# Block-sparse attention into a softplus feed-forward on one Trainium2 core: attention's pieces at five places of a feed-forward step in place of two

## The chip, the cores and the metric

One core of one Trainium2 chip. The metric is the device time of one execution in microseconds (us), the median of the runs shown. TensorE (PE in the profile) multiplies, VectorE (DVE) and ScalarE (ACT) work on elements, GpSimd (POOL) does so too and issues gathers, and SyncE (SP) issues most transfers.

## The reference

Attention over 4 batches, 8 heads, 768 positions and 64 values a head. A query block of 32 sees the key blocks beside it, the first and the last block, and three sampled ones; queries of the first and the last block see all. Its output is the input of a feed-forward pair with softplus between, with weights given as float64:

```python
def _attn_ref(q, k, v, sampled_blocks):
    scores = scale * np.matmul(q, k.transpose(0, 1, 3, 2))
    mask = np.abs(blk_i - blk_j) <= window
    mask = mask | (blk_i == 0) | (blk_j == 0) | (blk_i == n_blocks - 1) | (blk_j == n_blocks - 1)
...
    attn = np.exp(scores)
    attn = attn / (np.sum(attn, axis=-1, keepdims=True) + 1e-09)
    return np.matmul(attn, v)

def _moe_ref(x, w_in, w_out):
    h = x @ w_in
    g = np.maximum(h, 0.0) + np.log1p(np.exp(-np.abs(h)))
    return g @ w_out
```

x has 3072 rows of 512, w_in is 512 x 2048, w_out 2048 x 512.

## The kernel before

The rows of x are cut into 8 blocks of 384 (three groups of 128), the 2048 hidden columns into 16 slices of 128. A **feed-forward step** j is one row block t with one slice f. Steps 0 to 47 take slices 0 to 5 of all row blocks (phase 0) and leave partial sums in DRAM; steps 48 to 127 take slices 6 to 15 (phase 1) and add them. In a step `hidden` (line 230) makes twelve matmuls of 128x384: for each of four parts of the contraction high times high (L237), high weight times low input (L238), low times high (L239), since every float32 is held as a high and a low float32r half. ScalarE and VectorE make softplus of it over the next two steps, and three steps later (LEAD) `project` (line 284) makes nine output matmuls of 128x512, three for each group of rows (L293 to L295).

Attention is 28 sets (24 groups of four query blocks, and 4 sets of the blocks that see all keys) in two units each. A unit has three **pieces** (`pieces`, line 764): scores (L597 or L621; VectorE reads them out with a minimum, L603, L628), values (exponents on ScalarE, L653, for a later unit, then the matmuls L696 or L710), and transposes (L666, copied out by ScalarE L673 or VectorE L671). A set's output is turned (L741) and split into the high and low halves of x. For a set, keys are copied together: neighbours by VectorE (L493), the first and last block, called end keys, by `end_keys` (L476), sampled ones by GpSimd (L507). There are two buffers of gathered keys, two of values, four of PSUM with the tag "s", which the hidden tile, score tiles, transposes and turned outputs share, and three of PSUM for the outputs.

The float64 weights come as 64-bit integers (`load`, L148, 512 KB each) and are made float32 in small ticks between the pieces (`convert`, line 868): two ScalarE operations (L155, L159), three VectorE ones (L165, L172, L178) and an addition on GpSimd (L182). Slices 0 to 5 are split into halves at once (L189, L196); later ones go to DRAM (L201) and come back when attention's memory is free (`load_w2`, L897), where `split_w2` (line 899) makes the halves: a cast on ScalarE (L902) and a subtraction on GpSimd (L903).

Order: SP issues in program order. The other engines' order is set by a scheduler that goes by the program's order where it can. The program's order is the main loop from line 906: `first_half(j)` (L265 cast, L256 logarithm, hidden matmuls), then pieces as many as `due(j + 0.5)` asks for, then `second_half(j)` (L261, L271, the softplus rounding L248, L250, L251, and `project`), then pieces up to `due(j + 1.0)`. Three pieces come to a step. Before step 0 all pieces of the first row block run by themselves; with them, and until slices 0 to 5 are converted, ticks come at EARLY_TICKS = 1 for each piece and half step, later at LATE_TICKS = 0.5. `store` (line 306) copies a finished row block of outputs (`os`, L312) out of PSUM, on ScalarE and VectorE in turn.

Of the kernel before, what the change touches and what calls it, by code (L numbers as in the profile page):

```python
# [8 lines left out]
F32 = mybir.dt.float32  # L9
# [6 lines left out]
ALU = mybir.AluOpType  # L16
# [11 lines left out]
EARLY = 6  # L28

GROUPS = 3  # L30

LEAD = 3
# [18 lines left out]
def sparse_attention_ffn(  # L51
# [178 lines left out]
    def hidden(n):  # L230
        phase, t, f = seq[n]
        wh, wl = W[0, f]
        ph = ps_s.tile([P, 512], F32, tag="s", name=f"h{n}")[:, 0:TB]
        hi, lo = (X[phase, t][:, i] for i in range(2))
        for c in range(NC):
            cols = slice(c * P, (c + 1) * P)
            nc.tensor.matmul(ph, wh[:, cols], hi[:, c], start=(c == 0), stop=False)  # L237
            nc.tensor.matmul(ph, wh[:, cols], lo[:, c], start=False, stop=False)  # L238
            nc.tensor.matmul(ph, wl[:, cols], hi[:, c], start=False, stop=(c == NC - 1))  # L239
        e = gp.tile([P, TB], F32, tag="e", name=f"e{n}")  # L240
        nc.scalar.activation(e, ph, AF.Abs)  # L241
        nc.scalar.activation(e, e, AF.Exp, scale=-1.0)  # L242
        E[n] = (e, ph)
# [40 lines left out]
    def project(n):  # L284
        phase, t, f = seq[n]
        first, last = (f == (0, EARLY)[phase]), (f == (EARLY, NF)[phase] - 1)
        wh, wl = W[1, f]
        gh, gl = G.pop(n)
        for m in range(GROUPS):
            if first:  # L290
                po[m] = ps_o.tile([P, DM], F32, tag="o", name=f"o{phase}{t}_{m}")
            cols = slice(m * P, (m + 1) * P)
            nc.tensor.matmul(po[m], gh[:, cols], wh, start=first, stop=False)  # L293
            nc.tensor.matmul(po[m], gh[:, cols], wl, start=False, stop=False)  # L294
            nc.tensor.matmul(po[m], gl[:, cols], wh, start=False, stop=last)  # L295
        if last:
            store(phase, t)

# [139 lines left out]
    def load_queries(m):  # L438
        if m >= len(order):
            return  # L440
        b, g = order[m]
        qc[b, g] = wk.tile([P, NP, NI, BLOCK], F32, tag="qc", name=f"qc{b}_{g}", bufs=2)
        nc.sync.dma_start(out=qc[b, g], in_=q[b, g])
# [29 lines left out]
    def end_keys(m, copies):  # L473

        for copy, slot, blkno in zip(copies, (NR, 2 * NR + 1), (0, LAST)):
            copy(  # L476
                out=kg[m % 2][:, :, slot, :],
                in_=kT[order[m][0]][:, blkno : blkno + 1, :].to_broadcast([P, NI, NP * BLOCK]),
            )

    def gather_keys(m):
        b, g = order[m]
        ni = NI if g < NG - 1 else 2
        kd = kg[m % 2]

        def of_block(i):

            eng = (nc.vector if i < 2 else nc.scalar) if m == 0 else nc.gpsimd
            copy = nc.scalar.copy if m == 0 and i >= 2 else eng.tensor_copy
            if i == 0:  # L490
                at = kT[b][:, 4 * g : 4 * g + NR, :]
                pattern = [list(x) for x in at.ap]
                ins = nc.vector.tensor_copy(  # L493
                    out=kd[:, 0:ni, 0:NR, :].rearrange("p i s f -> p i (s f)"),
                    in_=bass.AP(at.tensor, at.offset, [pattern[0], [NP * BLOCK, ni], [1, NR * NP * BLOCK]]),
                )
                tc.keep_in_program_order(ins)
                if m % NG < 2:
                    first = nc.vector.tensor_copy if m == 0 else nc.scalar.copy
                    end_keys(m, (first, nc.scalar.copy) if m < 2 else 2 * (nc.gpsimd.tensor_copy,))  # L500
            (r,) = registers(eng, [2 * g + i // 2])
            for s in range(NR):
                x = nc.s_assert_within(
                    eng.snap((r >> (16 * (i % 2) + 5 * s)) & 31), 0, LAST,
                    skip_runtime_bounds_check_because="a sampled block is one of the key blocks",
                )
                copy(  # L507
                    out=kd[:, i, 1 + NR + s, :], in_=kT[b][:, bass.ds(x, 1), :].rearrange("p n f -> p (n f)")
                )

        key_work.extend((m, lambda i=i: of_block(i)) for i in range(ni))


# [328 lines left out]
    load_values(1)  # L842
    load_keys(2)
    scores(1)
    for h in range(weights.extra):
        weights.load(h)
    exponents(0)
    load_queries(2)
    transposes(0)
    exponents(1)  # L850
    spread_ends()
# [6 lines left out]
    def attend():  # L858
        nonlocal done
        attention[done]()  # L860
        done += 1
        gather()
        convert()
# [20 lines left out]
    def due(x):  # L884

        last, at = 0.0, needs[0]
        for t in range(1, NTB):
            end = t * EARLY - AHEAD
            if x <= end:
                return at + (needs[t] - at) * (x - last) / (end - last)  # L890
            last, at = end, needs[t]
        return len(attention)

    def load_w2(f):
        for which in range(2):
            W[which, f] = [pools["w2"].tile([P, DM], F32R, name=f"w{x}{which}{f}") for x in range(2)]
            nc.sync.dma_start(out=W[which, f][1].bitcast(F32), in_=wD[which, f])  # L897

    def split_w2(f, which):

        hi, lo = W[which, f]
        nc.scalar.copy(out=hi, in_=lo.bitcast(F32))  # L902
        nc.gpsimd.tensor_tensor(out=lo, in0=lo.bitcast(F32), in1=hi.bitcast(F32), op=ALU.subtract)  # L903

    ahead = None
    for j in range(len(seq) + LEAD):
        if j >= SECOND:
            t, f = seq[j][1:] if j < len(seq) else (NTB, -1)
            if f == EARLY + 2 and t + 1 < NTB:
                load_x(t + 1)  # L910
            if f == EARLY + 4:
                load_y(t)
        if j == SECOND - 3:
            load_x(0)
        first_half(j)
        while done < len(attention) and done < due(j + 0.5):
            attend()
        convert()
        second_half(j)
        while done < len(attention) and done < due(j + 1.0):  # L920
            attend()
        convert()
        if done == len(attention) and ahead is None:
            assert weights.done(), weights.at
            actx.close()
            pools["w2"] = ctx.enter_context(tc.tile_pool(name="w2", bufs=1, side="right"))
            ahead = EARLY
        while ahead is not None and ahead < min(NF, EARLY + 2 * (j + EARLY - SECOND + 1)):
            load_w2(ahead)
            ahead += 1  # L930

        for which in range(2):
            f = EARLY + j + 3 - SECOND - LEAD * which
            if EARLY <= f < NF:
                split_w2(f, which)


_BLOCKS = 24
# [35 lines left out]
```

## Time and profile before

| | before |
|---|---|
| median of 3 runs | 823.24 us (821.51 to 823.3) |
| the profiled execution, its own time | 830.36 us |
| its span, first to last instruction | 828.6 us |
| TensorE busy | 786.3 us (95%), 8108 matmuls |
| VectorE busy | 587.6 us (71%) |
| ScalarE busy | 485.8 us (59%) |
| GpSimd busy | 261.6 us (32%) |
| mean granted TensorE clock | 0.983 |
| HBM read, written | 97.85 MB, 30.41 MB |

Busy time is the time in which an engine works on at least one instruction. TensorE's matmuls overlap, so one that shows 0.34 us can be followed after 0.17 us: its pace is read from the starts. The shares are means over stretches with different limits, so stretches are looked at apart. The profiled execution took longer than the runs behind the median; differences are worked out within it.

### The profile page before, as it was taken

What the parts mean: (1) busy time and instruction counts of PE and PEld (TensorE: products, weight loads), DVE (VectorE), ACT (ScalarE), POOL (GpSimd) and SP (SyncE); (2) the same over time, 40 slices, a digit from 0 to 9 for tenths busy, and PEclk for the clock granted to TensorE, in tenths of its full rate; (3) what the DMA queues carried; (4) which work ended last, traced back from release to release, by engine and by line L of the source; (5) the groups of instructions that cost most, each with busy time, mean ns of one, the idle gap of its engine ahead of it and who ended that gap; (6) DMA issues with size and microseconds to landing.
All of it is one profiled execution on the core that took longest, in us unless ns stands there. A gap on an engine that the chain in (4) does not pass through costs nothing.

```text
span 828.6 us, 21424 instructions
## 1 busy us (share of the span) xinstructions
PE 786.3 (95%) x8108; PEld 651.7 (79%) x8108; DVE 587.6 (71%) x1454; ACT 485.8 (59%) x1170; POOL 261.6 (32%) x421
## 2 busy tenths in 40 slices
PE   8779969999999999999999999999999999999997
PEld 7546747776778767776778779999999999999996
DVE  5678999688787788886664886666656565656564
ACT  4776856766776766765664664444444444444442
POOL 6683886442666328464000670000000000000000
PEclk9799989999999999999999999999999999999999
DMA  8877698577697686955515461212121222222021
GB/s 246 237 221 265 199 243 290 173 236 251 183 296 224 215 278 181 286 147 167 204 40 190 143 240 64 102 52 97 57 88 65 77 76 77 77 77 77 0 77 39
DMA packets 48408, 129.66 MB, mean 156 GB/s; under 512 B 5488, under 2 KB 5616, under 8 KB 46256
## 3 DMA queue, kind: packets, MB, share of 16 engines
q1 hardware_dynamic: 42304, 109.79, 41.6%
q0 software_dynamic: 5712, 17.57, 7.5%
q8 instruction: 64, 1.05, 0.5%
q10 hardware_dynamic: 288, 0.93, 0.3%
q14 instruction: 40, 0.33, 0.1%
HBM read 97.85 MB, written 30.41 MB: 155 GB/s over the span
## 4 chain that ended last, share of the span: by engine, by line
PE 61%; DVE 18%; ACT 11%; issue 5%; DMA 3%; SPq 1%; another core or an unknown queue 1%; DVEq 0%; ACTq 0%
PE h L237 9%; PE o L293 8%; PE h L238 8%; PE h L239 8%; PE o L294 8%; PE o L295 8%; ACT pr L653 5%; PE t L666 3%; PE s L597 3%; PE x L696 3%; DVE e L250 2%; DVE pr L603 2%; DVE u L248 2%; DMA vg<-in_v_dram 2%; DVE wt L178 1%
## 5 line engine op out<-in xcount | busy, mean ns | idle before, releaser
L237 PE MATMUL h<-x,w 128*128 128x384 f32 x512 | 178.5, 349 | 4.4 <-DVE e L251 2.5
L238 PE MATMUL h<-x,w 128*128 128x384 f32 x512 | 173.9, 340 | 0.0
L239 PE MATMUL h<-x,w 128*128 128x384 f32 x512 | 173.5, 339 | 0.0
L293 PE MATMUL o<-w,gh 128*128 128x512 f32 x384 | 156.1, 407 | 2.9 <-DVE os L312 2.8
L248 DVE TENSOR_SCALAR u<-e 128x384 f32<-128x384 f32 x128 | 51.5, 402 | 145.3 <-ACT e L242 145.3
L295 PE MATMUL o<-w,gl 128*128 128x512 f32 x384 | 152.2, 396 | 0.0
L294 PE MATMUL o<-w,gh 128*128 128x512 f32 x384 | 151.7, 395 | 0.0
L241 ACT ACTIVATE e<-h 128x384 f32<-128x384 f32 x128 | 62.8, 491 | 126.2 <-PE h L239 125.8
L653 ACT ACTIVATE pr<-pr,nmax 128x256 f32<-128x256 f32 (+2 forms) x208 | 110.3, 532 | 44.0 <-DVE nmax L603 27.9
L237 PEld LDWEIGHTS h<-x,w 128*128 128x128 f32 x512 | 97.3, 190 | 14.8 <-DVE e L251 2.8
L265 ACT CAST gh<-u 128x384 fp32r<-128x384 f32 x128 | 65.4, 511 | 73.8 <-PE o L294 67.1
L563 POOL DMA_INDIRECT vg<-in_v_dram,ix x88 | 88.4, 1004 | 58.5 <-PE x L696 30.3
L238 PEld LDWEIGHTS h<-x,w 128*128 128x128 f32 x512 | 97.6, 191 | 3.6
L507 POOL COPY kg<-kT 128x128 f32 x252 | 84.9, 382 | 49.2 <-PE s L597 47.0
L239 PEld LDWEIGHTS h<-x,w 128*128 128x128 f32 x512 | 97.2, 190 | 0.0
L256 ACT ACTIVATE u<-u 128x384 f32<-128x384 f32 x128 | 66.9, 523 | 50.2 <-DVE e L250 41.5
L293 PEld LDWEIGHTS o<-w,gh 128*128 128x128 f32 x384 | 72.0, 188 | 24.8 <-issue 8.6
L295 PEld LDWEIGHTS o<-w,gl 128*128 128x128 f32 x384 | 72.1, 188 | 17.3
L603 DVE CUSTOM_DVE_ANT_1 pr<-s,mask 128x256 f32<-128x256 f32 (+1 forms) x192 | 69.6, 415 | 22.0 <-PE s L597 10.5
L250 DVE SCALAR_TENSOR_TENSOR e<-u,e 128x384 f32<-128x384 f32 x128 | 82.2, 642 | 3.8
L294 PEld LDWEIGHTS o<-w,gh 128*128 128x128 f32 x384 | 72.2, 188 | 13.4 <-issue 1.2
L261 DVE TENSOR_TENSOR u<-u,e 128x384 f32<-128x384 f32 x128 | 76.8, 600 | 2.9 <-ACT u L256 1.6
(82 smaller groups left out, 1128.1 us busy)
## 6 DMA issues: line engine op xcount, KB each, us to landing
vg<-in_v_dram SPq DMA_DIRECT2D x19, 768.0 KB
xD<-x SPq DMA_DIRECT2D x8, 1536.0 KB
x<-xD SPq DMA_DIRECT2D x8, 1536.0 KB
raw<-in_w_in_dram SPq DMA_DIRECT2D x16, 512.0 KB
raw<-in_w_out_dram SPq DMA_DIRECT2D x16, 512.0 KB
qc<-in_q_dram SPq DMA_DIRECT2D x24, 256.0 KB
vg<-in_v_dram SPq DMA_DIRECT2D x12, 512.0 KB
yD<-os SPq DMA_DIRECT2D x24, 256.0 KB
```

The source lines that it names most:

```text
L237: nc.tensor.matmul(ph, wh[:, cols], hi[:, c], start=(c == 0), stop=False)
L238: nc.tensor.matmul(ph, wh[:, cols], lo[:, c], start=False, stop=False)
L239: nc.tensor.matmul(ph, wl[:, cols], hi[:, c], start=False, stop=(c == NC - 1))
L250: nc.vector.scalar_tensor_tensor(out=e, in0=u, scalar=-1.0, in1=e, op0=ALU.add, op1=ALU.subtract)
L261: nc.vector.tensor_tensor(out=l, in0=l, in1=e, op=ALU.add)
L293: nc.tensor.matmul(po[m], gh[:, cols], wh, start=first, stop=False)
L294: nc.tensor.matmul(po[m], gh[:, cols], wl, start=False, stop=False)
L295: nc.tensor.matmul(po[m], gl[:, cols], wh, start=False, stop=last)
L507: copy(out=kd[:, i, 1 + NR + s, :], in_=kT[b][:, bass.ds(x, 1), :].rearrange("p n f -> p (n f)"))
L563: nc.gpsimd.indirect_dma_start(out=vd[0 : 3 * BLOCK, 1, i, :], out_offset=None, in_=v, in_offset=bass.IndirectOffsetOnAxis(ap=ix[:, b, 4 * ...
L603: nc.vector.tensor_tensor_reduce(out=pr[r][rows, j], in0=ps[r][rows, j], in1=mask[rows, g].unsqueeze(2).to_broadcast([ni * BLOCK, NS, BLOCK]),
L653: nc.scalar.activation(x, x, AF.Exp, bias=nmax[rows, r, j : j + 1], scale=-1.0, accum_out=rs[rows, h : h + 1])
```

## The change

There are five parts. `hidden` calls `between` after half of its matmuls, `project` after each group of rows but the last, and the main loop where it did before, so that pieces can come at five places of a step; `due` is as before, with finer values of its argument. `split_w2` subtracts on VectorE instead of GpSimd. Its calls take weights from a list sorted by when they are needed, one at an even step and two at an odd one from step 44 on. `end_keys` for the row groups behind the first two copies on ScalarE instead of GpSimd, 12 copies. And the first three float64 loads are issued behind the exponents of unit 0 and the queries of row group 2.

```diff
@@ hidden
             nc.tensor.matmul(ph, wl[:, cols], hi[:, c], start=False, stop=(c == NC - 1))
+            if c == NC // 2 - 1:
+                between(n + 0.25)
@@ project
             nc.tensor.matmul(po[m], gl[:, cols], wh, start=False, stop=last)
+            if m < GROUPS - 1:
+                between(n + LEAD + 0.5 + 0.5 * (m + 1) / GROUPS)
@@ gather_keys
-                    end_keys(m, (first, nc.scalar.copy) if m < 2 else 2 * (nc.gpsimd.tensor_copy,))
+                    end_keys(m, (first, nc.scalar.copy))
@@ start
     scores(1)
+    exponents(0)
+    load_queries(2)
     for h in range(weights.extra):
         weights.load(h)
-    exponents(0)
-    load_queries(2)
@@ new function
+    def between(x):
+
+        while done < len(attention) and done < due(x):
+            attend()
@@ split_w2
-        nc.gpsimd.tensor_tensor(out=lo, in0=lo.bitcast(F32), in1=hi.bitcast(F32), op=ALU.subtract)
+        nc.vector.tensor_tensor(out=lo, in0=lo.bitcast(F32), in1=hi.bitcast(F32), op=ALU.subtract)
@@ main loop
+    parked = sorted(later, key=lambda x: (x[0] + LEAD * x[1], x[1]))
...
-        while done < len(attention) and done < due(j + 0.5):
-            attend()
+        between(j + 0.5)
...
-        while done < len(attention) and done < due(j + 1.0):
-            attend()
+        between(j + 1.0)
...
-        for which in range(2):
-            f = EARLY + j + 3 - SECOND - LEAD * which
-            if EARLY <= f < NF:
-                split_w2(f, which)
+        for _ in range(1 + j % 2):
+            if j >= SECOND - 4 and parked:
+                split_w2(*parked.pop(0))
```

Lines behind line 239 have other numbers in the changed kernel: L293 to L295 become L295 to L297, L666 L670, L696 L700, L903 L912.

The first place is the end of step 18 on TensorE: output matmuls (o), turned output (y), values (x), transposes (t), then the next hidden matmuls (h). Before:

```order
L295 MATMUL o_2_3640<-w_2008,gl_3929 128x512
L741 MATMUL y_4086<-ident,xs_3990 128x128 x4
L696 MATMUL x_4092<-vg_174,pt_0_3995 32x64 x8
L696 MATMUL x_4092<-vg_174,pt_4_4002 32x64 x8
L696 MATMUL x_4092<-vg_174,pt_0_3995 32x64 x8
L696 MATMUL x_4092<-vg_174,pt_4_4002 32x64 x8
L666 MATMUL t_0_4127<-ident,pr_0_3898 128x128 x4
L666 MATMUL t_4_4134<-ident,pr_1_3899 128x128 x4
L237 MATMUL h_4146<-x_3_3121,w_1100 128x384
```

Now, the same place from the values' last rows on:

```order
L700 MATMUL x_4086<-vg_174,pt_0_3995 32x64 x8
L700 MATMUL x_4086<-vg_174,pt_4_4002 32x64 x8
L295 MATMUL o_1_3654<-w_2008,gh_3861 128x512
L296 MATMUL o_1_3654<-w_2009,gh_3861 128x512
L297 MATMUL o_1_3654<-w_2008,gl_3929 128x512
L295 MATMUL o_2_3688<-w_2008,gh_3861 128x512
L296 MATMUL o_2_3688<-w_2009,gh_3861 128x512
L297 MATMUL o_2_3688<-w_2008,gl_3929 128x512
L670 MATMUL t_0_4127<-ident,pr_0_3898 128x128 x4
L670 MATMUL t_4_4134<-ident,pr_1_3899 128x128 x4
L237 MATMUL h_4146<-x_3_3121,w_1100 128x384
```

The values now come behind the first group's three output matmuls, and six output matmuls stand between values and transposes. In the same step the scores moved from behind the twelve hidden matmuls to their middle. Counted over the whole program, TensorE's order goes from an attention matmul to a step's 86 times before and 142 times now, from a step's matmul into scores or values 58 and 72 times, and from one kind of attention matmul to another 121 and 63 times.

The second place is VectorE near step 42, where the second weights (w) are split. Before, it has the softplus rows alone:

```order
L248 TENSOR_SCALAR u_7127<-e_7121 128x384
L250 SCALAR_TENSOR_TENSOR e_7121<-u_7127,e_7121 128x384
L251 SCALAR_TENSOR_TENSOR e_7121<-h_7108,e_7121 128x384
L271 TENSOR_TENSOR gl_7172<-u_7086,gh_7152 128x384
L261 TENSOR_TENSOR u_7127<-u_7127,e_7121 128x384
```

Now:

```order
L912 TENSOR_TENSOR w_7141<-w_7141,w_7140 128x512
L250 TENSOR_SCALAR u_7127<-e_7121 128x384
L912 TENSOR_TENSOR w_7144<-w_7144,w_7143 128x512
L252 SCALAR_TENSOR_TENSOR e_7121<-u_7127,e_7121 128x384
L273 TENSOR_TENSOR gl_7172<-u_7086,gh_7152 128x384
L253 SCALAR_TENSOR_TENSOR e_7121<-h_7108,e_7121 128x384
L912 TENSOR_TENSOR w_7147<-w_7147,w_7146 128x512
L263 TENSOR_TENSOR u_7127<-u_7127,e_7121 128x384
L912 TENSOR_TENSOR w_7188<-w_7188,w_7187 128x512
L912 TENSOR_TENSOR w_7150<-w_7150,w_7149 128x512
```

The subtractions stand between the softplus operations of one step; seven come before VectorE's first copy of `os` behind that place, and further on four follow each other (w_7244 to w_7253).

The third place is SP's queue at the start: queries (qc) and float64 weights (raw). Before:

```order
L554 DMA vg_174<-in_v_dram 32x512 x2
L148 DMA raw_411<-in_w_in_dram 128x512
L148 DMA raw_413<-in_w_in_dram 128x512
L148 DMA raw_415<-in_w_in_dram 128x512
L443 DMA qc_2_422<-in_q_dram 128x512
L545 DMA vg_173<-in_v_dram 96x4x512
```

Now:

```order
L558 DMA vg_174<-in_v_dram 32x512 x2
L447 DMA qc_2_416<-in_q_dram 128x512
L148 DMA raw_418<-in_w_in_dram 128x512
L148 DMA raw_420<-in_w_in_dram 128x512
L148 DMA raw_422<-in_w_in_dram 128x512
L549 DMA vg_173<-in_v_dram 96x4x512
```

The queries, whose buffer has to come free first, went ahead of three loads.

## Rows read from the trace of the kernel before

**Rows 1.** Stretches: us, busy time (instructions) of PE, PEld, DVE, ACT, POOL; PEclk, DMA share, GB/s.

```profile
85.00:150.00 65.00, 55.32 (x761) 42.63 (x760) 60.94 (x141) 44.80 (x121) 48.29 (x73) 0.89 0.80 229
150.00:440.00 290.00, 281.64 (x4207) 217.98 (x4207) 222.82 (x636) 196.61 (x525) 131.90 (x228) 1.00 0.68 208
440.00:500.00 60.00, 56.38 (x305) 49.13 (x304) 46.91 (x68) 36.66 (x77) 29.21 (x20) 1.00 0.54 197
500.00:828.00 328.00, 324.39 (x1616) 291.78 (x1614) 197.75 (x407) 150.03 (x305) 0.00 (x0) 1.00 0.19 67
```

**Rows 2.** TensorE's waits, 150 to 440 us: what for, us in total, times, longest.

```profile
PE x L710 <- issue: 1.7, 4, 0.5
PE x L696 <- issue: 1.7, 4, 0.5
```

**Rows 3.** TensorE's waits, 440 to 500 us.

```profile
PE o L293 <- DVE os L312: 2.8, 2, 1.7
```

**Rows 4.** Timeline of TensorE, one step: start us, us, engine, line, operation.

```profile
245.53 0.42 PE L237 MATMUL h<-x,w 128*128 128x384 f32 x1
245.79 0.34 PE L238 MATMUL h<-x,w 128*128 128x384 f32 x1
245.96 0.34 PE L239 MATMUL h<-x,w 128*128 128x384 f32 x1
...
247.52 0.34 PE L239 MATMUL h<-x,w 128*128 128x384 f32 x1
247.79 1.09 PE L597 MATMUL s<-kg,qc 64*32 64x256 f32 x32
```

**Rows 5.** The same, output matmuls right behind values.

```profile
301.10 0.51 PE L293 MATMUL o<-w,gh 128*128 128x512 f32 x1
301.44 0.40 PE L294 MATMUL o<-w,gh 128*128 128x512 f32 x1
301.67 0.40 PE L295 MATMUL o<-w,gl 128*128 128x512 f32 x1
```

**Rows 6.** VectorE's groups, 455 to 500 us: busy us, mean ns | idle before.

```profile
L250 DVE SCALAR_TENSOR_TENSOR e<-u,e 128x384 f32<-128x384 f32 x10 | 10.5, 1046 | 0.3
L271 DVE TENSOR_TENSOR gl<-u,gh 128x384 fp32r<-128x384 f32 x10 | 8.7, 865 | 0.0
L261 DVE TENSOR_TENSOR u<-u,e 128x384 f32<-128x384 f32 x9 | 8.2, 915 | 0.1
L248 DVE TENSOR_SCALAR u<-e 128x384 f32<-128x384 f32 x10 | 6.8, 683 | 7.5 <-ACT e L242 7.5
```

**Rows 7.** VectorE's groups, 500 to 820 us.

```profile
L250 DVE SCALAR_TENSOR_TENSOR e<-u,e 128x384 f32<-128x384 f32 x76 | 42.4, 558 | 2.4
...
L248 DVE TENSOR_SCALAR u<-e 128x384 f32<-128x384 f32 x76 | 27.3, 359 | 110.2 <-ACT e L242 110.2
```

**Rows 8.** Groups of the whole span: subtractions and end keys.

```profile
L903 POOL TENSOR_TENSOR w<-w,w 128x512 fp32r<-128x512 f32 x20 | 29.2, 1495 | 45.4 <-DMA w<-wD 36.2 <-ACT w L902 9.2
...
L476 POOL COPY kg<-kT 128x512 f32<-128x512 f32 x12 | 12.7, 1071 | 7.7 <-DMA kT<-in_k_dram 7.7
...
L476 ACT COPY kg<-kT 128x512 f32<-128x512 f32 x3 | 1.8, 618 | 8.4 <-issue 8.4
```

**Rows 9.** Line L196: duration ns min/median/max, first and last start us.

```profile
L196 DVE TENSOR_TENSOR w<-wt,w x12: 673/686/1776, 50.8 to 136.4; 128x512 fp32r<-128x512 f32 x12
```

**Rows 10.** Line L493, the same columns.

```profile
L493 DVE COPY kg<-kT x24: 550/960/5264, 11.9 to 388.2; 128x1536 f32<-128x1536 f32 x20, 128x768 f32<-128x768 f32 x4
```

**Rows 11.** Timeline of VectorE near 111 us.

```profile
111.55 5.26 DVE L493 COPY kg<-kT 128x1536 f32<-128x1536 f32 x1
```

**Rows 12.** Timeline of SP's queue and of TensorE's weight loads at the start.

```profile
10.55 2.05 SPq L148 DMA_DIRECT2D raw<-in_w_in_dram  x3
22.18 0.33 SPq L443 DMA_DIRECT2D qc<-in_q_dram  x1
...
32.84 0.18 PEld L597 LDWEIGHTS s<-kg,qc 64*32 64x32 f32 x16 [0.17 <-POOL kg L507]
```

## The prediction

> **What bounds the kernel now.** I read the stretches first, then who waited for whom on TensorE, then single instructions. The first 85 us are attention alone and stand in no row here. [rows 1] splits the rest: from 85 to about 440 us attention's pieces lie between the feed-forward steps j=0 to 40, by 500 us the second weights are split, and behind that only feed-forward steps run. The reader is to compare TensorE's busy time with VectorE's. Behind 500 us TensorE is busy 324.4 of 328 us, and the change moves nothing there. From 150 to 440 us it is busy 281.6 of 290, so 8.4 us of idle time show. From 85 to 150 us it is busy 55.3 of 65, but VectorE 60.9: there VectorE sets the pace, since the float64 conversion runs there at its faster rate (EARLY_TICKS). From 440 to 500 us TensorE misses 3.6 us. The waits of TensorE name the rest: from 150 to 440 us, 3.4 us of the 8.4 are waits for nothing that the profile shows, inside the values' matmuls [rows 2]; from 440 to 500 us, 2.8 us are two waits for `os`, which VectorE and ScalarE copy out of PSUM [rows 3].
>
> So the room that the new places can reach is 8.4 - 3.4 = 5.0 us from 150 to 440 us; what else can be won lies with VectorE.
>
> **The change, part by part.**
>
> *Seams.* Splitting a feed-forward step into five parts makes TensorE go in and out of it more often. Each way costs. A step's hidden matmul that follows another starts 0.17 us after it (245.79 to 245.96); behind a transpose the first takes 0.26 us, and the last one ahead of scores 0.27 us instead of 0.17 [rows 4]. Behind the values the first output matmul takes 0.34 us against 0.23 [rows 5]. So a way out of attention costs about 0.10 us, and a way into scores or values as much; a way into transposes has no such row, and I take it at nothing, being of the same 128x128 shape. Counted in the two orders, ways from attention back to a step rise from 86 to 142, so 56 x 0.10 = 5.6 us; ways into scores or values rise from 58 to 72, 14 x 0.10 = 1.4 us. Against that, neighbours within attention fall from 121 to 63. What such a neighbourhood costs no row here isolates: if nothing, the sum is +7.0 us; if each of the 58 fewer costs the same 0.10, it is +1.2. I take +3.5, between them. About 8 of 41 steps lie where TensorE waits for VectorE anyway, so **+2.8 us**, between +1 and +7.
>
> *Waits that end.* With five places a unit's transposes come six output matmuls (6 x 0.23 = 1.4 us) behind the values instead of right behind them, and scores come in the middle of the hidden matmuls, so VectorE's and ScalarE's PSUM reads get more time before their slot is asked for again. The four slots of the "s" tag serve the hidden tile, both score tiles, both transposes and the turned output. The hidden tile is held 1 us longer, since scores now lie in its middle. Of the 5.0 us in reach I take **-3.5**, between 0 and -5.
>
> *The stretch where VectorE is the bound.* No VectorE instruction leaves it. But GpSimd slows VectorE: L493's copy takes 0.96 us in the median [rows 10] and 5.26 once, at 111.6 us [rows 11], in a stretch where VectorE has 4 us to spare. Four of the twelve end-key copies, 1.07 us each on GpSimd, lie in this stretch and go to ScalarE [rows 8]. If the one long copy does not fall in the same place, 4.3 us come back; if something else does, nothing. I take **-2**.
>
> *Splits on VectorE.* Twenty subtractions of 1.50 us leave GpSimd [rows 8] and cost VectorE 0.69 each by L196, the same operation on the same shape [rows 9]: 20 x 0.69 = 13.7 us more. While GpSimd subtracts, VectorE's own operations are slow: L250 takes 1.05 us, L271 0.87, L261 0.92, L248 0.68 [rows 6]; later, without GpSimd, L250 takes 0.56 and L248 0.36 [rows 7], and I take L271 and L261 as L250. The excess is 4.9 + 3.1 + 3.2 + 3.2 = 14.4 us. So VectorE's load stays (46.9 of 60 us in [rows 1]), 0.7 us lower. But a long subtraction no longer holds the queue for 1.5 us at a time, and VectorE's copy of `os`, for which TensorE waits, lies behind seven splits that now cost 0.69 each. I take half of the 3.6 us, **-1.8**, between -3.6 and +2: a split waits for its load and ScalarE's cast in VectorE's own queue, and behind it wait the softplus steps. [...]
>
> *End keys on ScalarE.* Twelve copies of 0.62 us [rows 8], 7.4 us in all, of which ScalarE's free time covers most (196.6 busy of 290, 44.8 of 65 [rows 1]); some wait there for the key blocks' DMA ahead of softplus operations. **+0.5**, between 0 and +7.4.
>
> *Float64 loads later.* On SP's queue the queries of row block 2 go ahead of three 512 KB loads. Before, the loads were issued at 10.6 us and the queries at 22.2, and the scores that need them ran at 32.8 us, held by the gathered keys and not by them [rows 12]. Now the three loads wait for the queries' buffer. I take **0**, between -2 and +2: earlier queries lie in the cover of the gathers, and if that cover is gone, the conversion's first loads are late next.
>
> Sum: 2.8 - 3.5 - 2 - 1.8 + 0.5 + 0 = -4.0 us. The profiled execution took 830.4 us, 7.1 above the median of the runs shown (823.24), so I expect 826.4 profiled and **819.2 us** as the median, if what the profile adds stays.
>
> **The rivals.** A difference under 0.3% (2.5 us) cannot be told from none by a measurement of this kernel.
>
> 1. *Gains and seams cancel.* The five places recover a third of the 5.0 us, the long copy is replaced by another, and VectorE's load is only shuffled: +2.8 - 1.7 - 0 - 1.8 + 0.5 = -0.2, near 823. For it: TensorE is already busy 97% from 150 to 440 us. Against it: the two waits for `os` have a plain cause. 0.27.
>
> 2. *Seams win (slower).* Place: TensorE's own order from 150 to 440 us, where it is the bound. All 56 ways out and 14 ways in cost 0.10, nothing comes back within attention, and the waits only move: +7.0 + 0.5 - 1.8 = +5.7, **828.9 us**. It decides as soon as less than about 3 us of waits end. For it: the cost is certain at each seam [rows 4, 5], the gain is not. Against it: transposes behind values pay for a seam today as well. 0.19. [...]
>
> 3. *The early stretch opens.* If evener work keeps TensorE from idling before 150 us, its clock stays up. [...] In that stretch TensorE had idled 9.7 of 65 us. [...] Against it: VectorE's 60.9 of 65 us hold the pace there whatever the clock. 0.12.
>
> That the change does not do what it says is excluded by the order: three pieces a step, as before, now in separate places.
>
> **How the numbers follow.** My forecast has 0.42, the rivals 0.27, 0.19 and 0.12. Faster is 0.42 + 0.12 = 0.54, the same 0.27, slower 0.19. The forecast alone spans 814 to 822: half of the open terms either way. The range to hold 8 in 10 reaches down past rival 3 (811) and up to most of rival 2 (828).
>
> **What would show it.** Right: from 150 to 440 us TensorE's waits for VectorE and ScalarE shrink under 2 us while hidden matmuls (L237) grow in mean; from 440 to 500 us L250 falls to about 0.56 us, the subtractions stand on VectorE at about 0.7 us, and TensorE's wait for `os` halves; from 85 to 150 us VectorE is still busy above 90%. Wrong: feed-forward steps as long as before and TensorE's idle time only named otherwise; VectorE waiting for ScalarE's casts or for the weights' DMA ahead of the splits; ScalarE waiting for the key blocks' DMA; or a clock of 1.00 already before 150 us, which would be rival 3.

## The result and the profile after

| | before | after |
|---|---|---|
| median of 4 runs | 822.38 us | 813.79 us |
| lowest and highest | 818.31, 823.3 | 807.65, 814.27 |
| the profiled execution, its own time | 830.36 us | 814.27 us |
| span | 828.6 us | 812.1 us |
| mean granted TensorE clock | 0.983 | 0.989 |

The ratio is 0.9883, with a 95% interval of 0.984 to 0.9925: 8.6 us faster, where 4.0 were forecast. The profiles differ by more, 16.5 us of span: the profiled execution of before, 830.36 us, lies above all four of its timed runs, that of after among its own. The experiments show what goes with that.

The stretches of the changed kernel, to be laid beside [rows 1]:

```profile
0.00:85.00 85.00, 70.42 (x1305) 52.68 (x1306) 63.53 (x216) 62.49 (x158) 56.99 (x115) 0.98 0.92 272
85.00:150.00 65.00, 58.10 (x800) 42.81 (x799) 61.36 (x148) 46.29 (x124) 44.89 (x69) 0.89 0.71 202
150.00:440.00 290.00, 285.27 (x4174) 220.89 (x4173) 214.94 (x632) 198.81 (x530) 121.42 (x207) 1.00 0.68 211
440.00:500.00 60.00, 60.00 (x302) 54.27 (x301) 46.97 (x96) 39.83 (x82) 0.00 (x0) 1.00 0.48 180
```

From 440 to 500 us TensorE no longer misses anything (56.38 busy before, 60.00 now), and VectorE, which now does the subtractions, is busy for as long as before (46.91 and 46.97). From 150 to 440 us TensorE's idle time fell from 8.4 to 4.7 us. VectorE still has little to spare from 85 to 150 us, and the granted clock there is 0.89 as before. (The stretches are cut by time, and attention ends some 12 us earlier now, so they do not hold quite the same work.)

Of the signs that the prediction named, four came as said: the time of L250 (L252 now, 0.553 us), the subtractions on VectorE, the waits for `os`, and VectorE's share from 85 to 150 us (61.36 of 65). From 150 to 440 us TensorE's named waits for VectorE and ScalarE add up to 3.4 us, where under 2 were expected (4.4 before); the hidden matmuls of L237 grew in mean, from 360 to 374 ns.

VectorE's groups from 440 to 485 us, the counterpart of [rows 6]:

```profile
L912 DVE TENSOR_TENSOR w<-w,w 128x512 fp32r<-128x512 f32 x20 | 13.1, 684 | 2.1 <-DMA w<-wD 2.1
L252 DVE SCALAR_TENSOR_TENSOR e<-u,e 128x384 f32<-128x384 f32 x11 | 6.1, 553 | 0.2
L263 DVE TENSOR_TENSOR u<-u,e 128x384 f32<-128x384 f32 x11 | 6.1, 551 | 0.2
L273 DVE TENSOR_TENSOR gl<-u,gh 128x384 fp32r<-128x384 f32 x11 | 6.0, 550 | 0.4 <-ACT gh L267 0.4
L250 DVE TENSOR_SCALAR u<-e 128x384 f32<-128x384 f32 x10 | 3.5, 355 | 2.9 <-ACT e L244 2.9
```

A subtraction takes 0.684 us, the forecast's 0.69, and the softplus operations beside it are as short as where GpSimd is idle [rows 7] (L252 here is L250 before, L250 here L248).

The copies of neighbours' keys and of end keys, by line (minimum, median, maximum in ns):

```profile
L497 DVE COPY kg<-kT x24: 550/961/1640, 12.0 to 373.8; 128x1536 f32<-128x1536 f32 x20, 128x768 f32<-128x768 f32 x4
L480 ACT COPY kg<-kT x15: 606/618/634, 10.2 to 313.8; 128x512 f32<-128x512 f32 x15
```

The 5.26-us copy of [rows 11] is gone, but another operation is drawn out in the same stretch. VectorE's L250, 0.36 us elsewhere, and GpSimd beside it:

```profile
121.03 4.80 DVE L250 TENSOR_SCALAR u<-e 128x384 f32<-128x384 f32 x1 [0.85 <-ACT e L244]
120.70 2.58 POOL L182 TENSOR_TENSOR wt<-wt,raw 128x512 int32<-128x512 int32 x2
123.22 3.36 POOL L511 COPY kg<-kT 128x128 f32 x12
```

VectorE's reads of scores stand behind it, and TensorE's transposes at 127.69 us wait 2.8 us for them. TensorE's waits of the whole span that concern the values, before (with the 1.7 us of L710 in [rows 2] besides) and after ("issue": a wait for nothing that the profile shows):

```profile
PE x L696 <- issue: 6.6, 12, 1.2
```

```profile
PE x L700 <- issue: 0.4, 1, 0.4
```

Of these 8.3 us, waits with no releaser in the midst of the values' matmuls, 0.4 are left. No part of the change alters the values' matmuls themselves, only where they stand, which is the first sign that the two profiles differ by more than the change.

### The profile page after: what moved, and what is told of

Its sections match the earlier page's. It is cut to its first block, busy times and chain, and to the rows that moved or that the text cites. A ratio compares the mean times of both kernels' runs of the same rounds, so it can differ in the third digit from the quotient of the medians.

```text
span 812.1 us, 21433 instructions
## 1 busy us (share of the span) xinstructions
PE 781.7 (96%) x8108; PEld 647.6 (80%) x8108; DVE 574.8 (71%) x1474; ACT 489.6 (60%) x1182; POOL 223.3 (27%) x389
## 4 chain that ended last, share of the span: by engine, by line
PE 82%; DVE 7%; ACT 6%; DMA 2%; issue 2%; POOL 0%; SPq 0%; ACTq 0%; DVEq 0%; POOLq 0%
PE o L295 11%; PE h L237 11%; PE o L297 10%; PE o L296 10%; PE h L238 10%; PE h L239 10%; PE s L601 5%; PE t L670 4%; PE x L700 4%; ACT pr L657 3%; PE warm L831 2%; DMA kT<-in_k_dram 1%; PE s L625 1%; DVE pr L607 1%; PE x L714 1%
## 5 line engine op out<-in xcount | busy, mean ns | idle before, releaser
L237 PE MATMUL h<-x,w 128*128 128x384 f32 x512 | 180.0, 352 | 0.4 <-DVE nmax L632 0.2
L250 DVE TENSOR_SCALAR u<-e 128x384 f32<-128x384 f32 x128 | 50.8, 397 | 155.8 <-ACT e L244 154.4
L295 PE MATMUL o<-w,gh 128*128 128x512 f32 x384 | 158.7, 413 | 0.0
L297 PE MATMUL o<-w,gl 128*128 128x512 f32 x384 | 152.0, 396 | 1.2 <-issue 1.0
L237 PEld LDWEIGHTS h<-x,w 128*128 128x128 f32 x512 | 96.6, 189 | 19.4 <-issue 11.2
L567 POOL DMA_INDIRECT vg<-in_v_dram,ix x88 | 90.3, 1027 | 65.9 <-PE x L700 39.1
L295 PEld LDWEIGHTS o<-w,gh 128*128 128x128 f32 x384 | 72.0, 188 | 19.9 <-issue 7.1
L297 PEld LDWEIGHTS o<-w,gl 128*128 128x128 f32 x384 | 72.1, 188 | 18.8 <-issue 1.5
L263 DVE TENSOR_TENSOR u<-u,e 128x384 f32<-128x384 f32 x128 | 73.6, 575 | 3.0 <-ACT u L258 2.4
L273 DVE TENSOR_TENSOR gl<-u,gh 128x384 fp32r<-128x384 f32 x128 | 73.0, 570 | 2.8 <-ACT gh L267 2.8
```

The lines of the kernel that those rows point to most:

```text
L263: nc.vector.tensor_tensor(out=l, in0=l, in1=e, op=ALU.add)
L273: nc.vector.tensor_tensor(out=gl, in0=l, in1=G[n].bitcast(F32), op=ALU.subtract)
L567: nc.gpsimd.indirect_dma_start(out=vd[0 : 3 * BLOCK, 1, i, :], out_offset=None, in_=v, in_offset=bass.IndirectOffsetOnAxis(ap=ix[:, b, 4 * ...
```

## The experiments

Each kernel was timed against the kernel before, in five rounds on the same chip. The four groups of runs fell on four chips, and the kernel before itself took 831.08, 832.27, 821.26 and 830.88 us on them. Gains against before in microseconds are worked out from the ratio.

**The parts alone (before at 831.08 us).** Each is the kernel before with one part of the change.

The later loads:

```diff
     scores(1)
+    exponents(0)
+    load_queries(2)
     for h in range(weights.extra):
         weights.load(h)
-    exponents(0)
-    load_queries(2)
```

> The kernel before with one part of the change: queries of row group 2 and unit 0's exponents ahead of the three float64 loads. In the profiles of the whole change step 0 starts 7.4 us earlier than before (59.2 us, 66.6 before). Theory (the gain is a sum, and the later loads carry its first part): step 0 starts 4 to 7 us earlier, all four engines' common pause that ended at 22.2 us is gone, and the time falls by 3 to 7 us, ratio 0.992 to 0.996. Rival (the pause is of that one profiled execution, as my prediction's 0 has it): time within 2 us of before, ratio 0.998 to 1.002, and step 0 near the same place in the profile.

Measured: 831.15 us, 0.9993 (0.9973 to 1.0013). The rival holds: on this chip the later loads are worth nothing. Hidden step 0 starts at 68.1 us in this profile (66.6 before), so here they bring none of the 7.4 us at the start of after's profile.

The splits:

```diff
-        nc.gpsimd.tensor_tensor(out=lo, in0=lo.bitcast(F32), in1=hi.bitcast(F32), op=ALU.subtract)
+        nc.vector.tensor_tensor(out=lo, in0=lo.bitcast(F32), in1=hi.bitcast(F32), op=ALU.subtract)
...
+        for _ in range(1 + j % 2):
+            if j >= SECOND - 4 and parked:
+                split_w2(*parked.pop(0))
```

> The kernel before with the second weights' subtractions on VectorE, in the new order of calls. Theory: TensorE's two waits for os near 445 to 455 us end, it is busy all of 440 to 500 us, steps 40 to 52 take 3.5 to 5 us less; ratio 0.994 to 0.996. Rival (the gain there comes only because the places have given VectorE a lead by then): waits for os stay at 2 us or more, ratio 0.998 to 1.001.

Measured: 827.33 us, 0.9954 (0.9929 to 0.998), 3.8 us. The stretch from 440 to 500 us of this kernel (columns as in [rows 1]):

```profile
440.00:500.00 60.00, 60.00 (x360) 53.59 (x360) 45.19 (x91) 37.80 (x80) 0.00 (x0) 1.00 0.59 217
```

TensorE misses nothing without the five places too, so the theory holds: all of the 3.6 us come back. From the start of step 40 to that of step 52 it is 51.1 us; in all eight profiles of kernels with the splits it is 51.0 or 51.1, in the six without 55.8 to 57.7. How GpSimd held up `os` stands in the trace of before (VectorE, GpSimd, and TensorE, which waits):

```profile
463.20 1.53 DVE L250 SCALAR_TENSOR_TENSOR e<-u,e 128x384 f32<-128x384 f32 x1
466.24 1.64 DVE L261 TENSOR_TENSOR u<-u,e 128x384 f32<-128x384 f32 x1
468.65 0.68 DVE L312 COPY os<-o 128x512 f32<-128x512 f32 x1
455.57 11.89 POOL L903 TENSOR_TENSOR w<-w,w 128x512 fp32r<-128x512 f32 x8 [36.18 <-DMA w<-wD]
469.39 0.50 PE L293 MATMUL o<-w,gh 128*128 128x512 f32 x1 [1.66 <-DVE os L312]
```

Beside eight subtractions VectorE's softplus operations take up to three times as long, and its copy of `os` comes behind them. New order and new engine were not tried apart.

The end keys:

```diff
-                    end_keys(m, (first, nc.scalar.copy) if m < 2 else 2 * (nc.gpsimd.tensor_copy,))
+                    end_keys(m, (first, nc.scalar.copy))
```

> The kernel before with the end keys of the later row groups copied on ScalarE, 12 copies. Theory (a part of nearly no weight): the 5.26-us copy of neighbours' keys on VectorE at 111.6 us may shrink, time within 2 us, ratio 0.998 to 1.002. Rival (GpSimd's copies beside VectorE's cost 4 us or more in the stretch where VectorE sets the pace): ratio 0.994 to 0.996. Other rival (ScalarE waits for the key blocks ahead of softplus): ratio above 1.003.

Measured: 827.26 us, 0.9962 (0.994 to 0.9984), 3.2 us: the first rival. Its stretch from 85 to 150 us, and the line of neighbours' keys:

```profile
85.00:150.00 65.00, 58.63 (x862) 44.53 (x857) 62.05 (x158) 52.35 (x140) 50.79 (x81) 1.00 0.83 236
```

```profile
L493 DVE COPY kg<-kT x24: 553/966/1175, 12.1 to 381.7; 128x1536 f32<-128x1536 f32 x20, 128x768 f32<-128x768 f32 x4
```

No copy takes over 1.175 us now. TensorE is busy 58.63 instead of 55.32 us, and the granted clock is 1.00 instead of 0.89. From the start of hidden step 4 to that of step 6 it is 19.0 us, 24.7 before. One other operation is drawn out here, by less: L724, 0.17 us in the median, takes 2.83 at 124.6 us. What stood beside the long copy before were not the end keys, which GpSimd had copied from 102.90 to 105.80 us, but work that came behind them:

```profile
111.08 1.32 POOL L182 TENSOR_TENSOR wt<-wt,raw 128x512 int32<-128x512 int32 x1
112.33 0.76 POOL L507 COPY kg<-kT 128x128 f32 x3
113.05 1.29 POOL L182 TENSOR_TENSOR wt<-wt,raw 128x512 int32<-128x512 int32 x1
114.30 3.09 POOL L507 COPY kg<-kT 128x128 f32 x9
```

That work is still GpSimd's. In this run VectorE's copy takes 0.95 us at 113.62 us beside nine copies like the last ones, and it is they that take long, 6.64 us instead of 3.09.

The five places:

```diff
             nc.tensor.matmul(ph, wl[:, cols], hi[:, c], start=False, stop=(c == NC - 1))
+            if c == NC // 2 - 1:
+                between(n + 0.25)
...
             nc.tensor.matmul(po[m], gl[:, cols], wh, start=False, stop=last)
+            if m < GROUPS - 1:
+                between(n + LEAD + 0.5 + 0.5 * (m + 1) / GROUPS)
```

> The kernel before with five places for attention's pieces and nothing else. Theory (sum of parts): steps 12 to 40 take 4 to 5 us less, as between the two profiles; TensorE's idle time from 150 to 440 us falls from 8.4 to about 5 us; time 3 to 5 us lower, ratio 0.994 to 0.996. Rival (seams eat the waits that end): ratio 0.998 to 1.003. Rival (the places carry the whole gain, early stretch included): ratio below 0.991.

Measured: 845.33 us, 1.0173 (1.0141 to 1.0205): 14 us slower, further off than any of the three expected. In its profile six VectorE operations take over 2 us and over twice their median, in that of before three. The longest of them on VectorE's timeline, and then GpSimd's (start, us):

```profile
93.80 6.23 DVE L165 TENSOR_SCALAR wt<-wt 128x512 f32<-128x512 f32 x1
99.95 0.55 DVE L273 TENSOR_TENSOR gl<-u,gh 128x384 fp32r<-128x384 f32 x1
```

```profile
92.08 2.17 POOL L480 COPY kg<-kT 128x512 f32<-128x512 f32 x1
94.22 4.05 POOL L511 COPY kg<-kT 128x128 f32 x17
98.24 1.26 POOL L182 TENSOR_TENSOR wt<-wt,raw 128x512 int32<-128x512 int32 x1
```

Behind an end-key copy come seventeen sampled-key copies and an addition without a gap, and L165, 0.43 us in the median, ends 0.5 us after them. That gave the next theory.

**Parts together (before at 832.27 us).** Places and keys, without the rest:

```diff
+            if c == NC // 2 - 1:
+                between(n + 0.25)
...
+            if m < GROUPS - 1:
+                between(n + LEAD + 0.5 + 0.5 * (m + 1) / GROUPS)
...
+                    end_keys(m, (first, nc.scalar.copy))
```

> The kernel before with five places and the end keys on ScalarE, without the splits and the later loads. Alone the places were 1.0173 and the keys 0.9962. Theory (the places pay only when GpSimd no longer copies end keys: with them there, its sampled-key copies come 17 in a row and hold one VectorE operation for 6.2 us, and TensorE's transposes wait 5.4 us for VectorE): the two together are 0.990 to 0.995, and steps 0 to 40 take 4 to 6 us less than with the keys alone. Rival (the parts add up): 1.0173 x 0.9962 = 1.0134, that is 1.010 to 1.017. Rival (the keys only repair what the places spoil): 0.996 to 1.001.

Measured: 836.49 us, 1.006 (1.0034 to 1.0087). Theory and rivals all miss: the places still cost beside the keys, 1.006 / 0.9962 = 1.0098 (two runs on two chips), though less than alone. One VectorE operation alone is over 2 us now (L196, 4.41), too little for a cost of 8 us.

The whole change with end keys on GpSimd:

```diff
-                    end_keys(m, (first, nc.scalar.copy))
+                    end_keys(m, (first, nc.scalar.copy) if m < 2 else 2 * (nc.gpsimd.tensor_copy,))
```

> The whole change, but the end keys of the later row groups stay on GpSimd. Theory (the places need the keys on ScalarE): slower than before, 1.0173 x 0.9954 = 1.013, that is 1.008 to 1.017, with steps 2 to 40 some 10 us longer than in the whole change. Rival (the places' loss came from the splits or loads that were missing beside them, not from the keys): 0.988 to 0.995, as the whole change or the keys' 0.4% above it.

Measured: 837.32 us, 1.006 (1.0036 to 1.0084), under the theory's range and far over the rival's. The keys are worth half a per cent here as well (1.0012 with them, below), no more, though seven VectorE operations are over 2 us without them and two with them.

The whole change with two places:

```diff
-            if c == NC // 2 - 1:
-                between(n + 0.25)
...
-            if m < GROUPS - 1:
-                between(n + LEAD + 0.5 + 0.5 * (m + 1) / GROUPS)
```

> The whole change with two places in place of five: keys, splits and loads stay. Theory (keys and splits add up, 0.9962 x 0.9954 x 0.9993): 0.9909, that is 0.988 to 0.994, so that the places themselves are worth 0.3% or less beside them. Rival (the places carry the change once the keys are moved): 0.994 to 0.998.

Measured: 822.65 us, 0.99 (0.9867 to 0.9933), as the product of the parts.

The changed kernel itself:

> The changed kernel once more, beside the others on one chip: 0.9883 was measured, 0.984 to 0.9925; I expect 0.986 to 0.991. Theory (the profile's 16.5 us was partly of that one execution): the difference of the profiles is smaller this time, 8 to 12 us, and step 0's start is what varies. Rival (the shorter start belongs to the change): step 0 starts at 59 to 60 us again.

Measured: 832.29 us, 1.0012 (0.9988 to 1.0037): on this chip the change gains nothing, and its interval does not touch that of the first comparison. Hidden step 0 starts at 71.1 us although the later loads are in place (59.2 in the first profile, 58.0 in that of the third run below). The profile differs from the first one of the same kernel by this (TensorE's waits of the whole span):

```profile
PE x L700 <- issue: 11.4, 22, 1.2
...
PE h L237 <- DVE e L253: 3.2, 5, 1.0
```

22 times a value matmul waits for nothing the profile shows, where the first profile had one such wait. What they look like (TensorE, one values piece), and the output matmuls behind it:

```profile
379.72 0.85 PE L700 MATMUL x<-vg,pt 128*32 128x64 f32 x32
381.67 0.23 PE L700 MATMUL x<-vg,pt 128*32 128x64 f32 x1 [1.11 <-issue]
382.39 0.22 PE L700 MATMUL x<-vg,pt 128*32 128x64 f32 x1 [0.49 <-issue]
383.11 1.11 PE L700 MATMUL x<-vg,pt 128*32 128x64 f32 x30 [0.51 <-issue]
...
384.75 0.63 PE L296 MATMUL o<-w,gh 128*128 128x512 f32 x1
385.17 0.63 PE L297 MATMUL o<-w,gl 128*128 128x512 f32 x1
...
391.12 0.39 PE L296 MATMUL o<-w,gh 128*128 128x512 f32 x1
391.35 0.40 PE L297 MATMUL o<-w,gl 128*128 128x512 f32 x1
```

A piece of 64 such matmuls that takes 1.0 us elsewhere in this trace (279.36 to 280.39 us) takes 4.4, and the output matmuls behind it start 0.42 us apart, 0.23 some microseconds later. VectorE is held up too. Scores and their first read by VectorE, in this profile and in the first one, same step:

```profile
283.91 1.10 PE L601 MATMUL s<-kg,qc 64*32 64x256 f32 x32
...
287.04 0.42 DVE L607 CUSTOM_DVE_ANT_1 pr<-s,mask 128x256 f32<-128x256 f32 x1 [1.71 <-PE h L239]
```

```profile
272.49 1.09 PE L601 MATMUL s<-kg,qc 64*32 64x256 f32 x32
...
273.81 0.38 DVE L607 CUSTOM_DVE_ANT_1 pr<-s,mask 128x256 f32<-128x256 f32 x1
```

The scores end at 285.0 us, VectorE has nothing else to do from 285.3 us on, and it starts at 287.0. TensorE's semaphore update for these scores stands in the trace at 287.02 us, 2.0 us after the last of their matmuls; in the first profile it came with their end, at 273.65 us. In this trace 72 of VectorE's 1224 updates are missing, and 48 times the next one recorded comes over 0.5 us after the operation's end; in the first profile one is missing and none is late. The ten profiles with pauses all have this (61 to 81 missing, 41 to 53 late), the four without at most one of either.

**The pauses, and which place costs (before at 821.26 us).** The changed kernel a third time:

> The changed kernel a third time. The first comparison gave 0.9883 with before at 822.4 us, the second 1.0012 with before at 832.3 us. In the second one's profile pieces of values stand still for 0.5 us and more at a time with no releaser (22 times, 11.4 us up to 440 us, against 0.4 us in the first profile), and VectorE's score reads start up to 1.7 us after the scores are done. Theory (these pauses belong to the chip that runs it, and the places lose where they come): where before takes 830 us or more, the ratio is 0.998 to 1.004 and the pauses are there; where before takes 820 to 824 us, it is 0.984 to 0.992 and they are not. Rival (the first comparison was a chance of few runs): 0.998 to 1.004 whatever before takes.

Measured: 809.59 us, 0.9857 (0.9829 to 0.9884), with 0.4 us of such waits: as the theory has it. The kernel with two places (diff as above):

> The whole change with two places in place of five, once more: 0.99 beside a before of 832.3 us. Theory: again 0.987 to 0.993 where before takes 830 us or more, that is 8 to 10 us under the whole change on the same chip; where before takes 820 to 824 us, the places cost nothing or gain, and the two are within 4 us. Rival (the places lose everywhere): the whole change is 6 us or more slower than this one in both cases.

Measured: 807.68 us, 0.9831 (0.98 to 0.9862), no such wait at all. The two are 1.9 us apart with overlapping intervals: without the pauses no gain or loss of the five places can be told. Their stretches, five places first:

```profile
85.00:150.00 65.00, 59.21 (x875) 43.93 (x876) 60.91 (x159) 49.73 (x136) 45.67 (x68) 0.95 0.75 217
150.00:440.00 290.00, 288.06 (x4132) 224.63 (x4131) 216.61 (x632) 201.09 (x531) 118.64 (x204) 1.00 0.69 213
```

```profile
85.00:150.00 65.00, 59.32 (x903) 45.70 (x898) 60.86 (x155) 50.07 (x138) 50.03 (x79) 0.97 0.80 228
150.00:440.00 290.00, 286.77 (x4123) 224.53 (x4122) 223.55 (x628) 201.04 (x529) 116.70 (x204) 1.00 0.69 213
```

TensorE idles 1.9 us of the 290 with five places and 3.2 with two, and hidden steps 12 to 40 take 249.3 and 249.6 us. But the first profile of five places, without pauses as well, idled 4.7 us and took 252.7, so single profiles do not show what the places end or cost. Two things hold in all of them. Hidden matmuls (L237) from 150 to 440 us are longer in mean with five places, 372 to 378 ns in six profiles, than with two, 358 to 361 in seven: the seams are there. And where five places stand beside end keys on ScalarE, one L196 operation of steps 0 to 4 takes 4.4 us (0.69 in the median) beside a chain of sampled-key copies, in four profiles of four; with two or four places none takes over 1.8. From the start of step 0 to that of step 4 it is 47.3 to 48.2 us in these four, 44.6 to 45.3 in the three profiles of the change with fewer places.

Four places, all but the middle of the hidden matmuls:

```diff
-            if c == NC // 2 - 1:
-                between(n + 0.25)
```

> The whole change without the place in the middle of the hidden matmuls; the two between the output groups stay, so four places. Theory (the middle place costs, since scores in it put VectorE's reads of them ahead of its reads of the hidden tile: TensorE's next hidden matmuls then waited 3.2 us for e in the second profile, 0.2 with two places): these waits fall under 1 us, and the ratio lies at the two-place kernel's, within 0.3%. Rival (the output places cost): the ratio lies at the whole change's. Rival (each place costs its seams): half way between.

Measured: 811.6 us, 0.9871 (0.9845 to 0.9897). The theory misses its number: without the middle place it is no faster than with it. It was not tested where it was needed, since the waits that it explains, 3.2 us for e, are only 0.5 us with five places on this chip. Four places are 3.9 us slower than two, hardly beyond the runs' spread, with five between them, so which place costs stays open.

**The keys once more (before at 830.88 us).**

> The kernel before with the end keys on ScalarE alone, once more, for a chip without the pauses. There keys, splits and later loads together gave 0.9831, 13.6 us of 821.3. Theory (the keys carry the larger part, by opening the stretch from 85 to 150 us where VectorE sets the pace): where before takes 820 to 824 us, the ratio is 0.987 to 0.991, and hidden step 0 starts within 1 us of 58.2 us, as in the kernels with later loads, so that the loads are worth nothing; from 440 to 500 us TensorE misses 2 to 4 us, which is what the splits give. Rival (the later loads carry it where no pauses cover them): 0.993 to 0.998, and step 0 starts 3 us or more behind 58.2 us. Where before takes 830 us or more: 0.994 to 0.998, as in the first run of this kernel.

Measured: 826.05 us, 0.9949 (0.992 to 0.9977), on a chip with pauses (7.8 us of them), so it repeats the first run of the keys, and what they give without pauses stays open.

The version that is best in all of this is the change without the five places: 0.99 with pauses, where the whole change has 1.0012, and 0.9831 without them, where the whole change has 0.9857, not to be told apart.

## Why the prediction was right, and where it was wrong

**The sign and the range** were right for the first comparison: 813.79 us lies in 811 to 828. It is 5.4 us under the forecast. The two parts that carry the gain are those that carried most of the forecast, each at about twice its size, and the largest single term, the waits that end, is not to be seen in the time. That the time lies in the range is in part luck: the forecast was worked out within an execution with 8.3 us of pauses and then set against runs that, by their times, had none of them.

**Seams and waits that end** (+2.8 and -3.5, together -0.7). Without pauses the five places come to +1.9 us in time, not to be told from 0: the sum was not wrong as far as can be told, and neither is rival 1, that gains and seams cancel, for this part. The terms by themselves are not measured: TensorE idles 3.2 us from 150 to 440 us with two places, 1.9 and 4.7 in two profiles with five. The step that failed is "the room that the new places can reach is 8.4 - 3.4 = 5.0 us": 3.4 us had been set aside for waits with no releaser, but what was left is more than the 3.2 us that the two-place kernel idles there without pauses, so -3.5 could not be had. Where there are pauses the places cost 1.0098 beside the keys and 1.0012 / 0.99 = 1.0113 beside the rest. That is more than the +7.0 us of rival 2's seams, and its cause is open. Against two places on the same chip the unexplained waits in the values go from 7.6 to 11.4 us and the waits of hidden matmuls for e from 0.8 to 3.2; but with the keys alone and with keys and places the former are 8.2 and 8.4 us, and the places cost there too, so more pauses are not the whole of it. The terms also left out that other pieces in other places make GpSimd's chains meet other VectorE operations, as L196 above. That transposes behind values paid for a seam already is in the trace of before: from 150 to 440 us the first transpose starts 0.15 us after the last value matmul of L696 (median of 24), as a hidden or output matmul behind values does (0.15, median of 8).

**The stretch where VectorE is the bound, and end keys on ScalarE** (-2 and +0.5, together -1.5). Measured together: -3.2 and -4.2 us in two runs of the keys alone. The mechanism was the one named, GpSimd's work drawing out a VectorE copy to 5.26 us [rows 11], but what lay beside it were additions and sampled-key copies; that the end keys ahead of them had moved them there is likely, not shown. The term was mis-sized for the keys alone: what fell in the same place there was one operation of 2.83 us, and the clock stayed up as in rival 3 (1.00 instead of 0.89 in that profile). In the profile of before the granted clock was 0.50 from 106.9 to 110.3, 120.5 to 127.4 and 144.4 to 147.8 us and 1.00 in the rest of 85 to 150 us; TensorE had stood still for 1.4 us from 104.2 us, 2.2 from 117.1 and 1.7 from 141.6. A full clock there would by [rows 1] be worth 65 x 0.11 = 7.2 us, an estimate that the low end of the range counts on; no run shows it, and the keys with a clock of 1.00 gave 3.2. In the whole change the reason for the half came true in the first profile: L250 took 4.80 us and the clock was 0.89. In the third run's profile no operation that starts from 85 to 150 us takes over 2 us, and the clock was 0.95.

**Splits on VectorE** (-1.8, half of 3.6). Measured -3.8, between -5.9 and -1.7, and TensorE's 3.6 us end entirely. The step that failed is the half; VectorE's load stayed as worked out. The reading of the wait was not quite right either: the long subtractions stood in GpSimd's queue, and `os` came late behind softplus operations that they drew out (L250 to 1.53 us, L261 to 1.64). VectorE's load as a whole stays, 46.9 and 47.0 of 60 us, but the time falls, because TensorE no longer waits for `os`.

**Float64 loads later** (0). Measured 0.9993, with an interval of 2 us either way: right on a chip with pauses. Without them the loads were not tried alone.

**"If what the profile adds stays."** The profile of before, 830.36 us, carries 8.3 us of unexplained waits in the values, 3.4 of them in [rows 2], as do the chips where before takes 831 us. Where it takes 821 or 822 us, the profiles of the change have 0.4 us of them or none; the kernel before itself was not profiled there. So the 7.1 us go with the pauses and are not the kernel's own; I argued within that execution, and so priced a room that the changed kernels do not show elsewhere.

**What stays open.** Keys, splits and loads together give 1.7% without pauses (0.9831) and 1.0% with them (0.99, or 3.2 + 3.8 + 0.6 = 7.6 us by their single runs). Which part grows was not measured; the keys' run for it fell on a chip with pauses. Each chip was used on one occasion, so whether the pauses belong to the chip, or to the occasion or the recording, is not shown.

## What to carry to other kernels

Compare a profile's own time with the runs before pricing its idle time: waits with no releaser can belong to the chip or the occasion it was taken on (in the values' matmuls 11.4 us of them in one profile of the changed kernel, 0.4 in two), and part of what a change gains or loses may too. Measure the parts of a change one by one and left out one by one, since a part that looks like the change's core (the five places) can be worth nothing while a line beside it carries the gain. Look for single instructions many times their median on an engine that is the bound, before the change and again after it, since another may be drawn out in their place: taking work off GpSimd that ran beside VectorE was worth more (3.2 us for the end keys, 3.8 for the splits) than a finer interleaving of TensorE (14 us slower alone, and no gain to be told without pauses).

## What the runs showed of the hardware

- **The same program on different chips.** The kernel before took 821.3 and 822.4 us in two comparisons and 830.9 to 832.3 us in three. In every profile that goes with the longer times, value matmuls pause with no releaser for 7.6 us or more in all; in the four that go with the shorter times, for 0.4 us or none. On the former, 41 to 53 of VectorE's semaphore updates also come over 0.5 us late, up to 2.8 us or more in each trace, and 61 to 81 are missing from the trace. Whether the recording of the trace makes the pauses is not shown: the runs of the changed kernel timed on such a chip are as long as the profiled one (832.5 us for that one, 832.3 the median), but every one of them left a span and a clock in the record, and no run here separates the recording from the chip.
- **GpSimd and VectorE.** A VectorE operation of 0.43 us took 6.23 us while GpSimd ran seventeen short copies and an addition without a gap; one of 0.96 us took 5.26 us and one of 0.36 us took 4.80 beside other such chains. Each ended within 0.8 us of the end of its chain.
- **TensorE after a pause.** After a values piece that stood still three times within 3 us (the second profile of the changed kernel), output matmuls started 0.42 us apart; 7 us later, 0.23 us apart. The granted clock was 1.00 from 374.0 to 379.7 us, before the pauses, 0.50 from 384.7 to 386.4 us, and 1.00 again from 387.4 us.
